# Setting up constants in a planned order: sparse attention and a multiplicative FFN on one Trainium2 core

## Chip, cores and metric

The kernel runs on one core of one Trainium2 chip (trn2). The metric is the device time of one launch in microseconds (us). The core's engines are named as the profile names them: PE (matrix products; its weight loads are listed as PEld), DVE (vector), ACT (scalar and activation), POOL (GpSimd) and SP, whose queue issues the DMA transfers. Each engine takes its own instructions in order and waits for others through semaphores.

## The reference

Two stages. The first is attention over 8 batches, 8 heads, 576 positions and a head size of 64. Heads 0 to 3 see the last 32 positions; heads 4 to 7 see the earlier positions that are congruent modulo 32. The second is an FFN on the 4608 tokens.

```python
scores = scale * np.matmul(q, k.transpose(0, 1, 3, 2))
rel = pos[:, None] - pos[None, :]
mask_local = (rel >= 0) & (rel < stride)                       # stride = 32
mask_strided = (rel >= 0) & (pos[None, :] % stride == pos[:, None] % stride)
attn = softmax(np.where(mask, scores, -1e9))                   # 4 heads each
x = (attn @ v).transpose(0, 2, 1, 3).reshape(B * S, H * D)     # 4608 x 512
a, b = x @ w1, x @ w2                                          # 512 -> 1024
out = ((a * b) @ w3) @ w_out                                   # 1024 -> 1024 -> 512
```

The kernel is given fp32 arrays and computes in fp16 with fp32 accumulation. It forms w3 @ w_out once (called w34) and uses that in place of the last two products.

## The kernel before, in words

**Two layers of code.** First come plain statements that build constants (lines 322 to 387). Then the kernel declares its work as operations of a `Plan`: each has a set of engines with a cost in ns for each, the operations it depends on, buffers that it takes and gives back (4 PSUM banks "f", 2 pairs "B", 7 staging tiles "stg", and others) and a rank. `Plan.order` (line 86) walks a clock: at each moment, each free engine takes the ready operation with the lowest rank. The sequence that comes out is then issued, and every instruction issued through `pin` keeps its place in its engine's program order. The planner's clock decides only this order; on the chip each instruction waits for its real operands. `busy` (line 95) holds the moment at which the planner lets each engine begin.

**Dummy matmuls.** When PE has nothing ready for the next 350 ns of the planner's clock, before 26 us of it, and more than one bank "f" is free, the planner puts in a `spin` (line 326): a 128x512 matmul on the first block of w34, which is zeroed beforehand. It costs the planner 432 ns before 7 us and 216 after.

**Constants.** POOL makes the identity `id16`, the local mask `maskL`, `sel` and `causal`. DVE zeroes the borders of `kTS` and `kTL`, makes `place` from `id16`, and fills columns D to P of the value tiles `v16L` and `v16S` (two of each, for even and odd batches) with ones, which make PV also sum the weights. Two small matmuls at line 371 make the strided mask: the first from `sel`, whose product times `causal` is `maskK`; the second from `place` and `maskK`, whose result is copied to `maskS`. From the masks come `biasL` and `biasS` (line 380). ACT copies the ones into the second value tiles (lines 385 and 387). Only the two mask matmuls are pinned; the order of the other constant instructions is left to the framework, which places them on each engine as the trace shows.

**Main work.** Loads (line 311, SP's queue) bring fp32 tiles into the seven staging tiles in the fixed order of `_loads`: two blocks of w3, q and k of the second group of batch 0, the remainder of batch 0's positions, q and k of the first group, values, another w3 block, four parts of w_out, and so on. POOL casts each to fp16 (line 308), in the same order, which frees the staging tile. On PE then follow:

- `tr` (line 552): transposes of a w3 block; `mm` (line 571): its product with w_out, evicted to w34.
- `T` (line 643): transposes of q and k for a pair of heads; `R` (line 596): the same for the last 64 positions.
- `S` (lines 677 and 686): scores. For the first four pairs a bias matmul adds the mask before ACT's exp; later pairs multiply by the mask after it.
- `X` (lines 724 and 734): weights times values (PV); then a normalisation on DVE, and for some pairs `U` (line 803), a transpose back.
- `a`, `b` (lines 838 and 854): x @ w1 and x @ w2 for tiles of 512 tokens, multiplied on DVE; `o` (line 874): times w34, evicted by ACT and stored.

Of the kernel before, what the change touches and what calls it, by code (L numbers as in the profile page):

```python
# [9 lines left out]
FP32 = mybir.dt.float32  # L10
FP16 = mybir.dt.float16
AF = mybir.ActivationFunctionType
ALU = mybir.AluOpType
# [37 lines left out]
class Plan:  # L51
# [34 lines left out]
    def order(self, slack=0, start=None, spin=None, first=("ACT", "DVE", "POOL")):  # L86
# [5 lines left out]
            for d in o.deps:  # L92
                d.succ.append(o)
        free = {k: [(0, i) for i in range(n)] for k, n in self.cap.items()}
        busy = dict(SP=800, POOL=4200, ACT=3200, DVE=6500, PE=1500)
        busy.update(start or {})
        avail = {e: [] for e in busy}
        for o in ops:
# [5 lines left out]
        t, left = 0, len(ops)  # L104
# [38 lines left out]
        while left:  # L143
            while rel and rel[0][0] <= t:
                w, k, i = heapq.heappop(rel)
# [14 lines left out]
            if busy["SP"] <= t and nxt < len(self.loads):  # L160
                o = self.loads[nxt]
# [10 lines left out]
            for e in ("PE", *first):  # L172
# [3 lines left out]
                for o in avail[e]:  # L176
                    r = ready(o, e)
# [25 lines left out]
                o = best[1]  # L203
# [40 lines left out]
            if nxt < len(self.loads):  # L244
                o = self.loads[nxt]
# [6 lines left out]
            t = min(later)  # L252
# [4 lines left out]
def kernel(  # L257
# [11 lines left out]
    nc = tc.nc  # L269
    cfg = CFG  # L270
    B, H, S, D = q.shape
# [3 lines left out]
    P = 128  # L275
# [7 lines left out]
    SQ, ST = 72, 8  # L283
    NM = 512
    NR = S - NM
    KB = 96
# [6 lines left out]
    psp = ctx.enter_context(tc.tile_pool(name="psp", bufs=1, space=bass.MemoryType.PSUM))  # L293
# [27 lines left out]

    pin(nc.scalar.preload_act_table_set("natural_log_exp_and_others"))
    w34 = consts.tile([P, KF, DM], FP16)
    nc.vector.memset(w34[:, 0, :], 0.0)

    def spin(key):
        ps = bank("f", key, [P, DM], FP32)
# [3 lines left out]
    kTL = consts.tile([P, 2, 32 + S + 32], FP16)  # L331
    kTS = consts.tile([P, 2, ST * KB + 32], FP16)
    v16L = [consts.tile([P, 4, LT, P], FP16, name=f"v16L{i}") for i in range(2)]
    v16S = [consts.tile([KB, 4, ST, P], FP16, name=f"v16S{i}") for i in range(2)]
    ptms = [consts.tile([P, 576], FP16, name=f"ptm{i}") for i in range(4)]
    nc.vector.memset(kTS, 0.0)
    nc.vector.memset(kTL[:, :, 0:32], 0.0)
    id16 = consts.tile([P, P], FP16)
    make_identity(nc, id16)

    idR = consts.tile([P, NR], FP16)
    nc.scalar.copy(out=idR.rearrange("p (g u t) -> p g u t", g=4, u=2),
                   in_=id16[:, 32:32 + NR].rearrange("p (t u g) -> p g u t", u=2, g=4))

    maskL = consts.tile([P, LQ], FP16)
    nc.gpsimd.memset(maskL, 1.0)
# [6 lines left out]
    sel = consts.tile([4, 18, 4], FP16)  # L353
# [4 lines left out]
    causal = consts.tile([SQ, SQ], FP16)  # L358
# [1 line left out]
    nc.gpsimd.affine_select(out=causal, in_=causal, compare_op=ALU.is_ge, fill=0.0, base=0,  # L360
                            pattern=[[1, SQ]], channel_multiplier=-1)
    place = consts.tile([SQ, KB], FP16)
    nc.vector.memset(place, 0.0)
    nc.vector.tensor_copy(out=place[0:64, 32:KB], in_=id16[0:64, 0:64])
    nc.vector.tensor_copy(out=place[64:SQ, 0:32].rearrange("k (i f) -> k f i", f=4)[:, 0], in_=id16[64:SQ, 64:SQ])
    maskK = consts.tile([SQ, SQ], FP16)
    maskS = consts.tile([KB, SQ], FP16)
    sel2 = sel.rearrange("r a b -> r (a b)")
    for i, (lhs, rhs, n) in enumerate(((sel2, sel2, SQ), (place, maskK, KB))):
        mps = psp.tile([P, 512], FP32, tag=f"f{i}", name="mps")  # L370
        pin(nc.tensor.matmul(mps[0:n, 0:SQ], lhs, rhs, start=True, stop=True))
        if i == 0:
            nc.vector.tensor_mul(maskK, mps[0:n, 0:SQ], causal)
        else:
            nc.vector.tensor_copy(out=maskS, in_=mps[0:n, 0:SQ])

    biasL = consts.tile([P, LQ], FP16)
    biasS = consts.tile([KB, SQ], FP16)
    for o, i in ((biasL, maskL), (biasS, maskS)):
        nc.vector.tensor_scalar(out=o, in0=i, scalar1=-1.0, scalar2=30000.0, op0=ALU.add, op1=ALU.mult)  # L380

    nc.vector.memset(v16L[0][:, :, :, D:P], 1.0)  # L382
    nc.vector.memset(v16L[0][0:32, :, 0, :], 0.0)
    nc.vector.memset(v16S[0][:, :, :, D:P], 1.0)  # L384
    nc.scalar.copy(out=v16L[1][:, :, :, D:P], in_=v16L[0][:, :, :, D:P])
    nc.vector.memset(v16L[1][0:32, :, 0, 0:D], 0.0)
    nc.scalar.copy(out=v16S[1][:, :, :, D:P], in_=v16S[0][:, :, :, D:P])

    xT = [consts.tile([P, NTOK], FP16, name=f"xT{cc}") for cc in range(4)]
    w1h = consts.tile([P, KM, DF], FP16)  # L390
# [6 lines left out]
    POOL = {"POOL": 1040}  # L397
# [14 lines left out]
        o.clean = clean if first else 0  # L412
        return o

    early = []

    def cast(name, key, dmas, eng, fn, deps=(), take=(), last=True, rank=10):
        if eng == POOL and len(early) < cfg.get("early", 0):
            eng = {"POOL": 1040, "DVE": 700, "ACT": 1048}
            early.append(key)  # L420
        return plan.op(name, eng, fn, deps=list(dmas) + list(deps), take=take,
                       give=[("stg", key)] if last else [], rank=rank, lock=True)

    CE = cfg.get("cast", {})
    w3c, woc, w1c, w2c, x16, x16op, vop = {}, {}, {}, {}, {}, {}, {}
    Top, Rop, Sop, PVop = {}, {}, {}, {}
# [72 lines left out]
    def load_vL(b, hp):  # L499
        vt = v16L[b % 2]  # L500
        hs = slice(2 * hp, 2 * hp + 2)
        key = f"vL{b}_{hp}"
        ds = []
        ds.append(dma(key, key, 1500, [P, 2, LT, D], lambda s: s[32:P].rearrange("p h t d -> p (h t) d"),
                      _ap(v, (b * H + 2 * hp) * S * D, [[D, LQ], [LQ * D, 2 * LT], [1, D]]), clean=0))
        cs = []
        for i, pr in enumerate((bass.ds(32, 32), bass.ds(64, 64))):
            def fn(e, pr=pr):
                copy(e, vt[pr, hs, :, 0:D], stg[key][pr])
            c = cast(f"c{key}{i}", key, ds, {"POOL": 825}, fn, last=(i == 1))  # L510
            late.append((c, lambda: [PVop.get((b - 2, h, g)) for h in (0, 1) for g in (0, 1)]))
            cs.append(c)
        hl = plan.op(f"h{key}", cfg.get("halo", {"POOL": 660}),
                     lambda e: copy(e, vt[0:32, hs, 1:LT, 0:D], vt[96:P, hs, 0:LT - 1, 0:D]),
                     deps=cs, rank=9, lock=True)
        late.append((hl, lambda: [PVop.get((b - 2, h, g)) for h in (0, 1) for g in (0, 1)]))
        for g in range(2):
            vop[(b, hp, g)] = cs + [hl]
# [23 lines left out]
    for jc in range(KF):  # L542
        js = bass.ds(jc * P, P)
        key = f"tr{jc}"

        def fn(e, jc=jc, key=key):
            if "w3T0" not in big:
                for i in range(2):
                    big[f"w3T{i}"] = ffn.tile([P, KF // 2, DF], FP16, tag="abt", bufs=4, name=f"w3T{i}")
            ps = bank("f", key, [P, KF, P], FP16)  # L550
            for kc in range(KF):
                pin(nc.tensor.transpose(ps[:, kc], big[f"w3_{jc}"][:, bass.ds(kc * P, P)], id16))  # L552

        t = plan.op(key, {"PE": 450}, fn, deps=[w3c[jc]],
                    take=[("f", key)] + ([("abt", "w3T0"), ("abt", "w3T1")] if jc == 0 else []),
                    give=[("w3n", f"w3_{jc}")], rank=cfg["frank"](jc) - 0.3)
        e0 = plan.op(f"w3T0_{jc}", {"DVE": 420, "ACT": 585},
                     lambda e, key=key, js=js: copy(e, big["w3T0"][:, :, js], bank("f", key)[:, 0:4]),
                     deps=[t], rank=5)
        e1 = plan.op(f"w3T1_{jc}", {"ACT": 585, "DVE": 420},  # L560
                     lambda e, key=key, js=js: copy(e, big["w3T1"][:, :, js], bank("f", key)[:, 4:8]),
                     deps=[t, e0], give=[("f", key)], rank=5)
        for nh in range(2):
            mk = f"mm{jc}_{nh}"
            ns = bass.ds(256 * nh, 256)
            h = None
            for hf in range(2):
                def fn(e, hf=hf, mk=mk, js=js, ns=ns):
                    ps = bank("f", mk, [P, 256], FP32) if hf == 0 else bank("f", mk)
                    for kc in range(4 * hf, 4 * hf + 4):  # L570
# [3 lines left out]
                h = plan.op(f"{mk}_{hf}", {"PE": 437}, fn, deps=[(e0, e1)[hf], woc[2 * nh + hf], h],  # L574
                            take=[("f", mk)] if hf == 0 else [], rank=cfg["frank"](jc + nh * cfg.get("nhr", 0)) - 0.1 * hf)
# [11 lines left out]
    prevPV = [None, None]  # L587
    xqs_t = {}
    ptm_t = {}
    for b in range(B):  # L590
        def fnR(e, b=b):
            ps = bank("f", f"R{b}", [P, 512], FP32)
            pv = ps.rearrange("x (i a c t) -> x i a c t", i=2, a=8, c=4)
            for i in range(2):
                for c in range(4):
# [4 lines left out]
                             rank=cfg["arank"](b, 0, "R"), soft=True)  # L600
        Rev = []
# [17 lines left out]
        for pi, hp in enumerate(cfg["pord"](b)):  # L619
# [51 lines left out]
            def fnS(e, hp=hp, nm2=nm2, w=w, m=m, kT=kT, kw=kw, local=local, pm=pm):  # L671
# [8 lines left out]
                for g in range(2):  # L680
                    sps = bank("B", f"S{nm2}_{g}")
                    for i in range(m):
                        ks, qs = kw * (g * m + i), w * (g * m + i)
                        for h in range(2):
# [2 lines left out]
                                                 qT[r_, hp, qs:qs + w], start=not pm, stop=not pm or i == m - 1))  # L687

            s = Sop[(b, hp)] = plan.op(f"S{nm2}", {"PE": (300 if local else 360) + 500 * pm}, fnS,
                                       deps=evs + Rev + prevPV, take=[("B", f"S{nm2}_0"), ("B", f"S{nm2}_1")],  # L690
                                       rank=rank("S"), soft=True, mode=1)
            for g in range(2):
                sk = f"S{nm2}_{g}"
# [43 lines left out]

                if old:
                    fp = fpo
                pv = PVop[(b, hp, g)] = plan.op(pk, {"PE": 246}, fp, deps=[mo] + vop[(b, hp, g)],  # L740
                                                take=[("B", pk)], rank=rank(f"P{g}"), soft=True)
                ptmu[pslot] = pv
                newPV[g] = pv
# [195 lines left out]
```

The softmax here doesn't subtract the row's maximum and nothing guards it: scores larger than these inputs give would overflow.

## Time and profile before

| | us |
|---|---|
| median of 6 runs | 281.04 (280.5 to 281.43) |
| the profiled execution, its time | 281.42 |
| its span in the trace | 279.7 |
| time outside the span | 1.72 |
| PE busy / DVE busy / ACT busy / POOL busy | 268.0 / 173.9 / 173.9 / 118.2 |
| DMA traffic, share of 16 engines | 48.65 MB, 57.2% (queue q1) |

The span runs from the first to the last instruction in the trace; the time of the execution is 1.72 us longer. In the page, busy time is the union of an engine's instruction times. Matmuls are pipelined, so that one matmul's row is longer than the distance to the next one's start: a full engine is seen by its having no idle time, and its pace by the distance of starts. In rows of groups or of the timeline, `out<-in` are the program's names of the tiles, followed by shapes and the number of instructions; the bracket tells how long the engine was idle before and what ended that. A cast's end is its start plus its length.

The first microseconds of the page's slices (40 slices of 7 us) show PE empty in the first and nearly full from the second on:

```profile
PE   0998999999999999999999999999999999999995
```

DVE builds constants in this time, as its timeline shows (start, length, engine, line):

```profile
1.32 0.72 DVE L336 MEMSET kTS<- 128x800 uint32 x1
2.01 0.09 DVE L337 MEMSET kTL<- 128x32 uint32 x1
2.05 0.10 DVE L363 MEMSET place<- 72x48 uint32 x1
2.41 1.34 DVE L382 MEMSET v16L<- 128x1536 f16 x1 [0.27 <-issue]
4.13 1.76 DVE L384 MEMSET v16S<- 96x2048 f16 x1 [0.38 <-issue]
5.89 0.27 DVE L383 MEMSET v16L<- 32x256 uint32 x1
6.13 0.17 DVE L386 MEMSET v16L<- 32x128 uint32 x1
6.23 0.48 DVE L364 COPY place<-id 64x64 f16<-64x64 f16 x1
6.72 0.17 DVE L365 COPY place<-id 8x8 f16<-8x8 f16 x1
6.92 0.19 DVE L380 TENSOR_SCALAR biasL<-maskL 128x96 f16<-128x96 f16 x1
7.02 0.22 DVE L373 TENSOR_TENSOR maskK<-mps,causal 72x72 f16<-72x72 f32 x1
7.55 0.23 DVE L375 CAST maskS<-mps 96x72 f16<-96x72 f32 x1 [0.31 <-PE mps L371]
7.82 0.18 DVE L380 TENSOR_SCALAR biasS<-maskS 96x72 f16<-96x72 f16 x1
```

### The profile page before, as it was taken

How to read it: one execution, taken by the hardware profiler on the slowest of the kernel's cores; microseconds unless marked ns; L12 is line 12 of the kernel's file. 1: busy time of each engine (PE TensorE's matmuls, PEld its weight loads, DVE VectorE, ACT ScalarE, POOL GpSimd, SP SyncE). 2: the span in 40 equal slices, each digit the busy share in tenths (PEclk: the TensorE clock that was granted, in tenths of full speed). 3: DMA queues.
4: the chain of work that ended last, by engine and by line, in shares of the span. 5: the costliest groups of instructions: out<-in, count | busy, mean ns of one | idle time of the engine just before them, and what ended most of it. 6: DMA issues, size and time to landing. Idle time of an engine off the chain costs nothing.

```text
span 279.7 us, 6299 instructions
## 1 busy us (share of the span) xinstructions
PE 268.0 (96%) x2434; PEld 151.7 (54%) x2434; DVE 173.9 (62%) x328; ACT 173.9 (62%) x321; POOL 118.2 (42%) x146
## 2 busy tenths in 40 slices
PE   0998999999999999999999999999999999999995
PEld 0566895746555555555555555555555544444443
DVE  7244756777678757875786778587857773320321
ACT  3454578775668866786677758865885675324321
POOL 6777997699579979550645073100000000000000
PEclk9999999999999999999999999999999999999999
DMA  6999999996999999978275300210020003003003
GB/s 235 355 357 297 364 356 353 266 267 216 301 269 309 302 302 290 273 209 272 82 193 168 147 1 2 98 56 2 1 113 39 2 0 152 1 0 150 0 2 150
DMA packets 53422, 48.65 MB, mean 174 GB/s; under 512 B 20752, under 2 KB 45584, under 8 KB 53392
## 3 DMA queue, kind: packets, MB, share of 16 engines
q1 hardware_dynamic: 53392, 48.24, 57.2%
q8 instruction: 19, 0.31, 0.5%
q14 instruction: 11, 0.09, 0.1%
HBM read 38.80 MB, written 9.44 MB: 172 GB/s over the span
## 4 chain that ended last, share of the span: by engine, by line
PE 95%; DVE 4%; issue 0%; ACT 0%; DVEq 0%
PE ps_o L874 23%; PE ps_b L854 22%; PE ps_a L838 22%; PE ps_T L643 5%; PE ps_mm L571 5%; PE ps_S L686 4%; PE ps_X L734 3%; PE ps_X L724 3%; PE ps_spin L328 2%; PE ps_U L803 2%; PE ps_tr L552 1%; DVE v16S L384 1%; PE ps_R L596 1%; PE ps_S L677 1%; DVE xqs L753 0%; DVE v16L L382 0%
## 5 line engine op out<-in xcount | busy, mean ns | idle before, releaser
L838 PE MATMUL ps_a<-xT,w1h 128*128 128x512 f16 x288 | 73.8, 379 | 0.0
L854 PE MATMUL ps_b<-xT,w2h 128*128 128x512 f16 x288 | 73.8, 379 | 0.0
L860 DVE TENSOR_TENSOR abt<-ps_b,asb 128x512 f16<-128x512 f32 x72 | 49.4, 689 | 39.3 <-PE ps_b L854 38.7
L874 PE MATMUL ps_o<-w,abt 128*128 128x512 f16 (+1 forms) x296 | 67.4, 374 | 0.0
L304 ACT COPY asb<-ps_a 128x512 f32<-128x512 f32 x72 | 42.2, 589 | 40.2 <-PE ps_a L838 39.4
L308 POOL CAST x<-st 128x1024 f16<-128x1024 f32 x32 | 32.9, 1038 | 34.3 <-PE ps_T L643 25.8
L854 PEld LDWEIGHTS <-w2h 128*128 128x128 f16 x288 | 26.9, 98 | 29.2
L874 PEld LDWEIGHTS <-abt 128*128 128x128 f16 x296 | 26.9, 98 | 27.7
L838 PEld LDWEIGHTS <-w1h 128*128 128x128 f16 x288 | 26.5, 98 | 26.6
L704 ACT ACTIVATE ps_S<-ps_S 96x576 f32<-96x576 f32 (+1 forms) x56 | 32.9, 628 | 11.0 <-PE ps_S L686 10.5
L304 ACT COPY osb<-ps_o 128x512 f32<-128x512 f32 x35 | 20.6, 588 | 18.5 <-PE ps_o L874 18.2
L790 DVE TENSOR_TENSOR xT<-ps_X,rcp 64x288 f16<-64x288 f32 x56 | 25.1, 449 | 5.6 <-ACT rcp L774 5.0
L308 POOL CAST v16L<-st 32x768 f16<-32x768 f32 (+1 forms) x32 | 26.3, 823 | 3.5 <-DMA st<-in_v_dram 1.9
L712 DVE TENSOR_TENSOR ptm<-ps_S,maskL 128x576 f16<-128x576 f32 x28 | 19.8, 751 | 12.0 <-ACT ps_S L704 12.0
L753 DVE TENSOR_TENSOR xqs<-ps_X,rcq 96x384 f16<-96x384 f32 (+1 forms) x36 | 20.5, 568 | 1.2
L712 DVE TENSOR_TENSOR ptm<-ps_S,maskS 96x576 f16<-96x576 f32 x28 | 19.8, 748 | 1.3 <-ACT ps_S L704 0.5
L308 POOL CAST v16S<-st 96x1024 f16<-96x1024 f32 x16 | 16.4, 1036 | 6.4 <-PE ps_X L724 6.4
L643 PE MATMUL ps_T<-id,x 128*128 128x128 f16 x256 | 19.1, 219 | 0.0
L774 ACT ACTIVATE rcp<-ps_X 64x576 f32<-64x576 f32 x28 | 18.1, 647 | 0.9
L763 ACT ACTIVATE ps_X<-ps_X 64x576 f32<-64x576 f32 x28 | 17.7, 631 | 0.9 <-PE ps_X L724 0.5
L306 DVE COPY qT<-ps_T 128x512 f16<-128x512 f16 x16 | 11.1, 692 | 9.6 <-PE ps_T L643 8.3
L734 PEld LDWEIGHTS <-ptm 128*96 128x96 f16 (+1 forms) x224 | 14.2, 123 | 4.3
(80 smaller groups left out, 279.3 us busy)
## 6 DMA issues: line engine op xcount, KB each, us to landing
out_dram<-osb SPq DMA_DIRECT2D x35, 256.0 KB
st<-in_moe_w_dram SPq DMA_DIRECT2D x16, 512.0 KB
st<-in_q_dram SPq DMA_DIRECT2D x16, 512.0 KB
st<-in_k_dram SPq DMA_DIRECT2D x16, 512.0 KB
st<-in_v_dram SPq DMA_DIRECT2D x16, 288.0 KB
st<-in_v_dram SPq DMA_DIRECT2D x16, 256.0 KB
st<-in_moe_w_out_dram SPq DMA_DIRECT2D x4, 512.0 KB
st<-in_q_dram SPq DMA_DIRECT2D x8, 128.0 KB
```

Source lines behind the costliest of these rows:

```text
L304: pin(nc.scalar.copy(out=out, in_=in_))
L308: pin(nc.gpsimd.tensor_copy(out=out, in_=in_))
L643: pin(nc.tensor.transpose(ps[:, c * P:(c + 1) * P], x16[(b, x, hp // 2)][:, c, h0:h0 + 2] .rearrange("p h d -> p (h d)"), id16))
L704: pin(nc.scalar.activation(out=sps, in_=sps, func=AF.Exp, bias=0.0, scale=scale))
L712: pin(nc.vector.tensor_mul(ptm[0:kr, 0:576].rearrange("p (h a x) -> p h a x", h=2, x=w), pte[0:kr].rearrange("p h (a x) -> p h a x", x=w), ...
L734: pin(nc.tensor.matmul(xps[0:w, h, i * 65:(i + 1) * 65], ptms[pslot][0:kr, c0:c0 + w], vt[0:kr, 2 * (hp % 2) + h, g * m + i, 0:D + 1], sta ...
L753: pin(nc.vector.tensor_mul(xqs[0:w, 0:m].rearrange("p i h d -> p h i d"), xv[:, :, :, 0:D], _ap(rcp, 0, [[rcp.ap[0][0], w], [4, 2], [1, m] ...
L790: pin(nc.vector.tensor_mul(o, i0, i1))
L838: pin(nc.tensor.matmul(ps, w1h[:, ci, js], xT[ci][:, tok], start=(ci == 0), stop=(ci == KM - 1)))
L854: pin(nc.tensor.matmul(ps, w2h[:, ci, js], xT[ci][:, tok], start=(ci == 0), stop=(ci == KM - 1)))
L860: pin(nc.vector.tensor_mul(big[("abt", t)][:, jc, :], bank("f", f"b{t}_{jc}"), live[("asb", t, jc)]))
L874: pin(nc.tensor.matmul(ps, big[("abt", t)][:, ci, bass.ds(ts * P, P)], w34[:, ci, bass.ds(pt * nw, nw)], start=(ci == 0), stop=(ci == KF - ...
```

## The change

The constants on DVE, ACT and PE become operations of the plan, and their instructions are pinned. POOL's constants stay as they are; an operation `pl` of zero length stands for their end. The planner's start times for POOL, ACT and DVE are set to 3000, 2150 and 1300 ns. Since the mask matmuls are now planned, dummy matmuls can stand ahead of them and between them. S of the first four pairs depends on the biases, and each PV on the ones of its value tile. The helper `on` and its table `ALT` allow a cast to be put on another engine by configuration; the configuration names none. The `early` count, which was 0, goes.

```diff
-        busy = dict(SP=800, POOL=4200, ACT=3200, DVE=6500, PE=1500)
+        busy = dict(SP=800, POOL=3000, ACT=2150, DVE=1300, PE=1500)
...
-    nc.vector.memset(w34[:, 0, :], 0.0)
+    pin(nc.vector.memset(w34[:, 0, :], 0.0))
...
-    nc.vector.memset(kTS, 0.0)
-    nc.vector.memset(kTL[:, :, 0:32], 0.0)
...
-    nc.vector.memset(v16L[0][:, :, :, D:P], 1.0)
-    nc.vector.memset(v16L[0][0:32, :, 0, :], 0.0)
-    nc.vector.memset(v16S[0][:, :, :, D:P], 1.0)
-    nc.scalar.copy(out=v16L[1][:, :, :, D:P], in_=v16L[0][:, :, :, D:P])
-    nc.vector.memset(v16L[1][0:32, :, 0, 0:D], 0.0)
-    nc.scalar.copy(out=v16S[1][:, :, :, D:P], in_=v16S[0][:, :, :, D:P])
+    def first_dve(e):
+        pin(nc.vector.memset(kTS, 0.0))
+        pin(nc.vector.memset(kTL[:, :, 0:32], 0.0))
+        pin(nc.vector.memset(place, 0.0))
+        pin(nc.vector.tensor_copy(out=place[0:64, 32:KB], in_=id16[0:64, 0:64]))
+        pin(nc.vector.tensor_copy(out=place[64:SQ, 0:32].rearrange("k (i f) -> k f i", f=4)[:, 0],
+                                  in_=id16[64:SQ, 64:SQ]))
+
+    def mask_mm(key, lhs, rhs, n):
+        def fn(e):
+            pin(nc.tensor.matmul(bank("f", key, [P, 512], FP32)[0:n, 0:SQ], lhs, rhs, start=True, stop=True))
+        return fn
...
+    def ones(e, i, local):
+        t = v16L[i] if local else v16S[i]
+        if i == 0:
+            pin(nc.vector.memset(t[:, :, :, D:P], 1.0))
+        else:
+            pin(nc.scalar.copy(out=t[:, :, :, D:P], in_=(v16L if local else v16S)[0][:, :, :, D:P]))
+        if local:
+            pin(nc.vector.memset(t[0:32, :, 0, 0:D] if i else t[0:32, :, 0, :], 0.0))
+
+    pl = plan.op("pool", {"POOL": 0}, lambda e: None)
+    d0 = plan.op("init", {"DVE": 1300}, first_dve)
+    plan.op("idR", {"ACT": 310}, lambda e: pin(
+        nc.scalar.copy(out=idR.rearrange("p (g u t) -> p g u t", g=4, u=2),
+                       in_=id16[:, 32:32 + NR].rearrange("p (t u g) -> p g u t", u=2, g=4))))
+    m0 = plan.op("mk0", {"PE": 100}, mask_mm("mk0", sel2, sel2, SQ), deps=[pl, d0], take=[("f", "mk0")], rank=-200)
+    d1 = plan.op("maskK", {"DVE": 230}, lambda e: pin(
+        nc.vector.tensor_mul(maskK, bank("f", "mk0")[0:SQ, 0:SQ], causal)), deps=[m0], give=[("f", "mk0")])
+    m1 = plan.op("mk1", {"PE": 100}, mask_mm("mk1", place, maskK, KB), deps=[d1], take=[("f", "mk1")], rank=-200)
+    d2 = plan.op("maskS", {"DVE": 230}, lambda e: pin(
+        nc.vector.tensor_copy(out=maskS, in_=bank("f", "mk1")[0:KB, 0:SQ])), deps=[m1], give=[("f", "mk1")])
+    biases = [plan.op("bias", {"DVE": 190}, bias(*x), deps=[y]) for x, y in (((biasL, maskL), pl),
+                                                                            ((biasS, maskS), d2))]
+    onesop = {}
+    for local, c0, c1 in ((False, 1780, 1900), (True, 1620, 1500)):
+        onesop[(0, local)] = plan.op("ones", {"DVE": c0}, lambda e, local=local: ones(e, 0, local), deps=[d2], rank=1)
+        onesop[(1, local)] = plan.op("ones", {"ACT": c1}, lambda e, local=local: ones(e, 1, local),
+                                     deps=[onesop[(0, local)]], rank=8)
...
-                                       deps=evs + Rev + prevPV, take=[("B", f"S{nm2}_0"), ("B", f"S{nm2}_1")],
+                                       deps=evs + Rev + prevPV + biases * pm, take=[("B", f"S{nm2}_0"), ("B", f"S{nm2}_1")],
...
-                pv = PVop[(b, hp, g)] = plan.op(pk, {"PE": 246}, fp, deps=[mo] + vop[(b, hp, g)],
+                pv = PVop[(b, hp, g)] = plan.op(pk, {"PE": 246}, fp, deps=[mo, onesop[(b % 2, local)]] + vop[(b, hp, g)],
```

More of the change, by code (lines that the diff above doesn't have):

```diff
@@ L341 @@
     idR = consts.tile([P, NR], FP16)
-    nc.scalar.copy(out=idR.rearrange("p (g u t) -> p g u t", g=4, u=2),
-                   in_=id16[:, 32:32 + NR].rearrange("p (t u g) -> p g u t", u=2, g=4))
     maskL = consts.tile([P, LQ], FP16)
@@ L362 @@
     place = consts.tile([SQ, KB], FP16)
-    nc.vector.memset(place, 0.0)
-    nc.vector.tensor_copy(out=place[0:64, 32:KB], in_=id16[0:64, 0:64])
-    nc.vector.tensor_copy(out=place[64:SQ, 0:32].rearrange("k (i f) -> k f i", f=4)[:, 0], in_=id16[64:SQ, 64:SQ])
     maskK = consts.tile([SQ, SQ], FP16)
     maskS = consts.tile([KB, SQ], FP16)
[L368 to L375, printed above, removed]
@@ L377 @@
     biasL = consts.tile([P, LQ], FP16)
     biasS = consts.tile([KB, SQ], FP16)
-    for o, i in ((biasL, maskL), (biasS, maskS)):
-        nc.vector.tensor_scalar(out=o, in0=i, scalar1=-1.0, scalar2=30000.0, op0=ALU.add, op1=ALU.mult)
-    nc.vector.memset(v16L[0][:, :, :, D:P], 1.0)
-    nc.vector.memset(v16L[0][0:32, :, 0, :], 0.0)
-    nc.vector.memset(v16S[0][:, :, :, D:P], 1.0)
-    nc.scalar.copy(out=v16L[1][:, :, :, D:P], in_=v16L[0][:, :, :, D:P])
-    nc.vector.memset(v16L[1][0:32, :, 0, 0:D], 0.0)
@@ L387 @@
-    nc.scalar.copy(out=v16S[1][:, :, :, D:P], in_=v16S[0][:, :, :, D:P])
+    sel2 = sel.rearrange("r a b -> r (a b)")
+    def first_dve(e):
[5 more added lines that the diff above has]
+                                  in_=id16[64:SQ, 64:SQ]))
@@ new lines, in mask_mm, with bias @@
+    def mask_mm(key, lhs, rhs, n):
+        def fn(e):
+            pin(nc.tensor.matmul(bank("f", key, [P, 512], FP32)[0:n, 0:SQ], lhs, rhs, start=True, stop=True))
+        return fn
+    def bias(o, i):
+        return lambda e: pin(nc.vector.tensor_scalar(out=o, in0=i, scalar1=-1.0, scalar2=30000.0, op0=ALU.add,
+                                                     op1=ALU.mult))
+    def ones(e, i, local):
[6 more added lines that the diff above has]
+            pin(nc.vector.memset(t[0:32, :, 0, 0:D] if i else t[0:32, :, 0, :], 0.0))
@@ L413, in dma, with on @@
         return o
-    early = []
+    ALT = {1040: {"DVE": 700, "ACT": 1048}, 1048: {"DVE": 700, "ACT": 1048}, 1230: {"DVE": 800, "ACT": 1200},
+           825: {"DVE": 560, "ACT": 810}, 660: {"DVE": 590, "ACT": 700}}
+    def on(key, eng):
+        x = cfg.get("ce", {}).get(key)
+        return {x: (POOL["POOL"] if x == "POOL" else ALT[min(eng.values())][x])} if x else eng
     def cast(name, key, dmas, eng, fn, deps=(), take=(), last=True, rank=10):
[L418 to L421, printed above, removed]
+        return plan.op(name, on(name[1:], eng), fn, deps=list(dmas) + list(deps), take=take,
                        give=[("stg", key)] if last else [], rank=rank, lock=True)
@@ L512, in load_vL @@
             cs.append(c)
-        hl = plan.op(f"h{key}", cfg.get("halo", {"POOL": 660}),
+        hl = plan.op(f"h{key}", on(f"h{key}", {"POOL": 660}),
                      lambda e: copy(e, vt[0:32, hs, 1:LT, 0:D], vt[96:P, hs, 0:LT - 1, 0:D]),
```

## The prediction, made before the changed kernel was built

> **What bounds the kernel now.** I read the engine table over three windows, then the waits, the chain of waits of the first 24 us, and the timeline. First the windows: length, then busy us (instructions) of PE, PE weight load, DVE, ACT and POOL, the granted clock, DMA share and GB/s.
>
> ```profile
> 0.00:23.50 23.50, 15.14 (x154) 9.26 (x155) 11.03 (x24) 11.48 (x19) 16.94 (x30) 1.00 0.94 326
> 23.50:269.50 246.00, 245.92 (x2247) 138.67 (x2244) 161.37 (x301) 160.66 (x300) 101.31 (x117) 1.00 0.56 162
> 269.50:279.70 10.20, 6.96 (x41) 3.72 (x38) 1.54 (x3) 1.76 (x3) 0.00 (x0) 0.99 0.27 103
> ```
>
> From 23.5 us on PE has 0.08 us of idle time in 246 us, so nothing can be won there except by starting it earlier. Everything that PE lacks lies in the first 23.5 us. The longest PE wait there, and the chain (start, us, what):
>
> ```profile
> PE mps L371 <- DVE maskK L373: 4.2, 1, 4.2
> ```
>
> ```profile
> 2.41 1.34 DVE v16L L382
> ...
> 4.13 1.78 DVE v16S L384
> ...
> 6.30 0.41 DVE place L364
> ...
> 7.30 0.22 PE mps L371
> 7.52 3.89 PE ps_spin L328 x9
> 11.41 0.85 PE ps_tr L552 x8
> ...
> 13.45 2.59 PE ps_spin L328 x12
> 16.04 0.46 PE ps_T L643 x8
> ```
>
> PE's queue is in order and both mask matmuls stand at its head. The second needs `place` and `maskK`; DVE makes them only after it has filled v16L and v16S with ones, so PE stands until 7.30. Behind it come nine dummy matmuls, 0.43 us each, then the first w3 transposes, more dummies, and the first attention transposes (T) at 15.88. None of this waits for data:
>
> ```profile
> 9.55 1.04 POOL L308 CAST x<-st 128x1024 f16<-128x1024 f32 x1 [0.44 <-DMA st<-in_k_dram]
> ...
> 15.88 1.06 PE L643 MATMUL ps_T<-id,x 128*128 128x128 f16 x16
> ```
>
> T's operands were ready at 9.55 + 1.04 = 10.59; it ran 5.29 us late. The question is how much of this a later limit takes back. I matched every POOL cast, in order, with the first PE row that reads it. The tightest pair:
>
> ```profile
> 25.94 1.04 POOL L308 CAST w3n<-st 128x1024 f16<-128x1024 f32 x1 [1.54 <-PE ps_mm L571]
> ...
> 29.55 1.06 PE L552 MATMUL ps_tr<-id,w3n 128*128 128x128 f16 x16
> ```
>
> The row at 29.55 is two blocks of eight transposes 0.055 us apart; the second block (29.99) reads the fifth w3 cast, ready at 26.98: 3.01 us of slack. The row's "PE" is misleading: the semaphore of this cast's DMA rose at 25.79, long after the transposes that free its buffer, so the cast follows the DMA stream, whose share is 0.94 over the first window. The next tightest: the sixth w3 cast (33.29, read at 36.45: 3.2), the local value halo (29.64, read at 32.97: 3.3), the seventh w3 cast (34.27, 37.59: 3.3), batch 1's remainder (37.36, 40.75: 3.4). From the FFN weights on it is over 4 us, from batch 3 on over 9. So PE runs at least 3.0 us behind its data everywhere.
>
> **The change, part by part.**
>
> *DVE's order.* kTS, kTL and `place` now come first, the fills with ones after `maskS`. From DVE's first row at 0.94: 0.27 + 0.72 + 0.09 + 0.10, then the copies 0.48 + 0.17, with start gaps about 2.9. The first mask product was done at 3.08 already and `causal` is ready at 2.96, so maskK (0.22) ends near 3.4, the second mask matmul (0.22) near 3.8, instead of 7.52: 3.7 us off the head of PE's queue. The fills (1.76 + 1.34 + 0.27 + 0.17 = 3.5) follow maskS and the biases (0.23 + 0.18 + 0.19) and end near 8. Their cover: DVE's first other row stands at 12.30, and the evictions of the first w3 transposes, now due near 6.5, may go to ACT and are first read by the products of line 571, which need wo (first cast done at 17.80). Cost 0; without that cover at most the 1.8 us of one fill. ACT's two copies of ones (1.90 + 1.46) likewise end near 11, before its first T eviction near 11.7; if they slide later, each can hold up an exp by up to its 1.9 us.
>
> One rule speaks against this part. The row: the `place` copy of 64x64 took 0.48 us and ended at 6.71, as the POOL cast beside it ended at 6.68; a larger one-input DVE row (biasL, 128x96) took 0.19. The Trainium skill, "SBUF — State Buffer", section "Who interferes with whom", says that a DVE copy in a two-port mode and GpSimd lock each other out for a whole instruction. The copy now meets POOL's mask selects (0.24 to 0.37 each, the last ending at 2.96). By the row it stays 0.48; by the rule it could wait until 2.96 and end at 3.2, or push a select by as much. I take 0.48; either way 0.3 us lies under the dummies.
>
> *Dummies ahead of the masks.* PE can begin when w is zeroed (1.21) rather than at 7.33. About four 0.43 us dummies fit before 3.1, one between the mask matmuls, three before the first w3 transposes (cast ready at 5.16). They cost at most one dummy, 0.43, of delay, all before 10.59. Do they gain by warming? In the trace dummies start 0.427 us apart until about 13.1 and 0.216 after, although the clock column says 1.00 throughout: 5.8 us of work before full rate. The skill ("TensorE: Matmul & The Clock Gate", "What's actually happening") gives 3.4 us in a free-running window and closes the gate again after an idle window. Counting from 1.3 us, the row puts full rate at 7.1, the rule (one to two windows, my estimate) at 4.7 to 8.1. Both are before T. Were the gate still closed at 8 (the mask gaps counting as idle), some 11 dummies would cost 11 x 0.21 = 2.3 us more, and T would come at 12.4, still 3.5 early. I take 0.
>
> *PE after that.* T at 10.7 (was 15.88, 5.2 earlier); R behind its cast (11.71) at 11.8; its evictions end near 13.6; the first S near 13.7 (was 18.95). The second pair's T needs the cast ending at 14.30 (was 19.32: 4.9 earlier); PV needs v16S at 15.28 (was 20.22: 4.8); the normalisations and second S follow, so U ends near 19.0 (was 23.67). The products of line 571 then need wo3 (20.82) and wo1 (22.27) and run about 4.3 earlier. Then the fifth w3 cast holds: 26.98 plus 0.1 from cast to PE gives 27.08 instead of 29.99, **2.9 us earlier**. Every later slack is larger, so the 2.9 reaches the end.
>
> *Planner.* The new start times (POOL 3000, ACT 2150, DVE 1300) and the constants as planned operations can redraw the static orders. The trace has no row for this. Bounds: a better order fills the hole before 27.08 and is stopped by the next slacks, -4.0; a worse one leaves PE standing, bounded above only by the rivals below. Nearest is the order the trace shows, so 0. The new dependencies (S on biases, PV on ones) are met by 8 us, against S at 13.7. `on` and ALT are inert: CFG has no "ce" entry and early was 0. No DMA is added, moved or removed; SP's queue is the same.
>
> Sum against the profiled execution: span 279.7 - 2.9 = 276.8; its time 281.42 - 2.9 = 278.5. The median shown, 281.04, is 0.38 below that execution, so I forecast **278.1**.
>
> **Rivals.**
> 1. *Better order* (PE fills the hole before 27.08): gain 3.3 to 4.2, say 277.2. For: the hole is about 1.4 us. Against: S of the first local pair needs the normalisation behind it.
> 2. *The cover is gone.* The 5 us of lateness hid every eviction and arrival misjudged in the order; without it small PE waits return between 10 and 45 us and half is lost: 1.5 gained, 279.5. Against: the slacks above are measured arrivals.
> 3. *Hidden anyway or not done*: arrivals after 23 us set the end, 281.0. Against: 3.0 us of slack at every load.
> 4. *Slower.* An instruction needing a late cast is ordered into PE's queue ahead of work that is ready: for instance the last w3 block (cast 45.14) ahead of the first FFN products (ready at 40.3) holds PE 4.8 us. Before 27 us such a stand costs little, since PE must wait for the fifth w3 cast anyway; after it, one longer than 2.9 makes the kernel slower: with 4.8, 281.0 + 1.9 = 282.9. For: the lists are redrawn as a whole, and a stand this long was invisible while PE was late.
>
> **How the numbers follow.** Chances: forecast 0.62 (277.6 to 278.6), better order 0.12, cover gone 0.11, hidden 0.05, slower 0.10. Faster by over 0.2% (0.56 us, about what a measurement can tell): 0.62 + 0.12 + 0.11 = 0.85; same 0.05; slower 0.10. The range 277.0 to 280.4 leaves out the far part of the better order (0.03), hidden and slower (0.15).
>
> **What would show it.** Right: no DVE wait over 1 us on PE's second mask matmul, dummies from 1.3 us, T at 10.6 to 10.9, the fifth w3 block right behind its cast at 27.1, PE full from there, the last row 2.9 earlier. Wrong: T later than 12.5 (clock or fills), POOL casts later than before (the port), or PE gaps after 27 us (order).

## The result, and the profile after

The changed kernel takes 279.53 us (median; 278.51 to 281.89 in 31 runs) against 280.78 us (279.8 to 281.55 in 68 runs): ratio 0.9963, 95% interval 0.9953 to 0.9972. It is faster by 1.0 us by the ratio, 1.25 by the medians. Forecast was 2.9. The profiled executions differ by more than the medians: 279.06 us with a span of 277.3, against 281.42 with 279.7. Two executions in the experiments below, 305.82 us at a granted clock of 0.88 (experiment 3) and 288.71 us at 0.95 (kernel before), ran in a slower state of the chip and are left out of the medians and ratios.

The windows of the changed kernel (columns as before):

```profile
0.00:23.50 23.50, 18.05 (x184) 10.92 (x185) 13.31 (x27) 12.37 (x20) 16.32 (x29) 1.00 0.93 325
23.50:267.00 243.50, 242.59 (x2212) 135.63 (x2210) 159.78 (x298) 159.87 (x298) 101.95 (x118) 1.00 0.56 164
```

PE is busy 2.9 us more in the first window, and it now stands idle 0.91 us after it, where it had 0.08. Apart from 1.3 us at the very start, until w is zeroed, its largest waits in the first 30 us are (in total, times, longest):

```profile
PE ps_tr L575 <- POOL w3n L308: 2.1, 4, 0.9
PE ps_mm L594 <- POOL woh L308: 1.1, 1, 1.1
PE ps_spin L328 <- DVE w3T L306: 0.9, 1, 0.9
```

No wait for the masks is left. PE waits for casts of loaded data, and once for a bank that DVE frees late because the fills with ones stand in front (the third line; the part on DVE's order below says why they stood there so late). In time, from the timeline:

```profile
1.27 1.89 PE L328 MATMUL ps_spin<-w 128*128 128x512 f16 x4 [1.27 <-DVE w L324]
...
3.75 0.22 PE L375 MATMUL ps_mk<-maskK,place 72*96 72x72 f16 x1
...
10.74 1.06 PE L666 MATMUL ps_T<-id,x 128*128 128x128 f16 x16
...
26.35 1.04 POOL L308 CAST w3n<-st 128x1024 f16<-128x1024 f32 x1 [1.16 <-DMA st<-in_moe_w_dram]
...
27.45 0.62 PE L575 MATMUL ps_tr<-id,w3n 128*128 128x128 f16 x8 [0.91 <-POOL w3n L308]
```

The second mask matmul is issued at 3.75 and T at 10.74, 5.14 us earlier than before. The fifth w3 block stands directly behind its cast: ready at 26.35 + 1.04 = 27.39, read at 27.45. The chain of waits goes back from there not to DVE but to the stream of loads:

```profile
17.07 9.14 DMA st<-in_moe_w_dram
...
26.35 1.05 POOL w3n L308
...
27.45 0.62 PE ps_tr L575 x8
```

The engine line of the chain was "PE 95%; DVE 4%" before; it is now:

```profile
PE 89%; DMA 7%; POOL 1%; SPq 1%; issue 0%; DVE 0%; POOLq 0%; DVEq 0%
```

So the mechanism is the one forecast, down to the block that holds PE. The size is not.

### The profile page after: what moved, and what is told of

It is laid out like the page before. It is cut to its first block, busy times and chain, and to the rows that moved or that the text cites. A ratio compares the mean times of both kernels' runs of the same rounds, so it can differ in the third digit from the quotient of the medians.

```text
span 277.3 us, 6298 instructions
## 1 busy us (share of the span) xinstructions
PE 267.7 (97%) x2433; PEld 150.3 (54%) x2433; DVE 174.6 (63%) x328; ACT 174.0 (63%) x321; POOL 118.3 (43%) x146
## 4 chain that ended last, share of the span: by engine, by line
PE 89%; DMA 7%; POOL 1%; SPq 1%; issue 0%; DVE 0%; POOLq 0%; DVEq 0%
PE ps_o L897 23%; PE ps_b L877 23%; PE ps_a L861 22%; PE ps_T L666 5%; DMA st<-in_moe_w_dram 5%; PE ps_S L709 4%; PE ps_mm L594 3%; PE ps_X L757 3%; PE ps_X L747 3%; PE ps_U L826 2%; DMA st<-in_k_dram 2%; SPq L311 1%; PE ps_tr L575 1%; POOL w3n L308 1%; PE ps_R L619 1%; POOL v16S L308 0%
## 5 line engine op out<-in xcount | busy, mean ns | idle before, releaser
L594 PE MATMUL ps_mm<-woh,w3T 128*128 128x256 f16 x128 | 15.9, 272 | 1.1 <-POOL woh L308 1.1
```

Source lines behind the costliest of these rows:

```text
L594: pin(nc.tensor.matmul(ps, big[f"w3T{kc // 4}"][:, kc % 4, js], big["woh"][:, kc, ns], start=(kc == 0), stop=(kc == KF - 1)))
```

## The experiments

**A constant to read all of them by.** In every profile of the kernel before, the time less the start of the fifth w3 block on PE was 251.41 to 251.45 us, and the time less the start of the first T was 265.52 to 265.55. After that block PE is full, so each microsecond by which it starts later is a microsecond at the end. In these six profiles (the first, one in experiment 1, four in experiment 7) it starts when PE gets to it; in the changed kernel it starts when its data is there.

**1. Both kernels again.** No edit; one profile each.

> The kernel before, unchanged, profiled once more. Landing theory (after the change PE follows the casts, and the end moves with the landings between 20 and 34 us; before it, PE is late by its dummies, whose pace depends on when the PE clock opens): the time moves with the start of the first attention transposes T, which was 15.88 in the profile at 281.42 us, so about 265.5 us plus that start; a typical run has T nearer 15.2. The landing of the first local value tile (27.05 in the first profile) scatters by half a microsecond or more without moving the time. Contention theory (the change itself makes the casts after 20 us later): that landing stays within 0.2 us of 27.05.

> The changed kernel, unchanged, profiled once more. Landing theory: its time is about 251.3 us plus the landing of the first local value tile (27.76 at 279.06 us), and this landing differs from 27.76 by some tenths up to 1 us either way. Contention theory: the landing is again 27.7 or later, and at least 0.5 later than in the kernel before on the same chip.

Measured: 280.65 for the kernel before, T at 15.12 (265.5 + 15.12 = 280.6), the fifth w3 cast ready at 27.88, not 26.98. The changed kernel took 281.13 us, more than every profile of the kernel before but the first. Its timeline:

```profile
28.61 1.04 POOL L308 CAST w3n<-st 128x1024 f16<-128x1024 f32 x1 [1.01 <-DMA st<-in_moe_w_dram]
...
29.70 0.62 PE L575 MATMUL ps_tr<-id,w3n 128*128 128x128 f16 x8 [1.43 <-POOL w3n L308]
```

The same program, the same order, T at 11.77, and the fifth w3 cast ready at 29.65 instead of 27.39. 251.43 + 29.70 = 281.13: the landing is the time. I had tied the time to the first local value tile's landing; the fifth w3 block describes it better. Only the first profile of the changed kernel stands off, by 0.18 us (279.06 - 27.45 = 251.61), most of it from a later cast, the sixth w3 block, ready at 34.00 and read at 34.06. The marks named beforehand did not decide between the theories. The cast of the first local value tile began at 27.99 in the kernel before (27.17 in its first profile), so it scatters, as the landing theory has it. In the changed kernel it began at 29.71, 1.7 us later on the same chip: that is the mark of the contention theory, and more than the landing theory allowed.

**2. DVE's order alone.** The kernel before, constants pinned in the new order, everything else as it was; all dummies thus stand behind the masks.

```diff
-    nc.vector.memset(place, 0.0)
-    nc.vector.tensor_copy(out=place[0:64, 32:KB], in_=id16[0:64, 0:64])
+    pin(nc.vector.memset(place, 0.0))
+    pin(nc.vector.tensor_copy(out=place[0:64, 32:KB], in_=id16[0:64, 0:64]))
...
-    nc.vector.memset(v16L[0][:, :, :, D:P], 1.0)
+    pin(nc.vector.memset(v16L[0][:, :, :, D:P], 1.0))
```

> Kernel before with DVE's constants pinned in the new order alone (kTS, kTL, place, masks, biases, then the ones); planner, start times and dummies as before, so that all dummies stand behind the mask matmuls. Landing theory: masks done near 3.8, nine dummies from there, T near 11.8 (11.4 to 12.7) instead of 10.7; the later waits for data absorb this, so the time is that of the changed kernel: 1.0 to 1.3 us under before (ratio 0.995 to 0.997). Rival (dummies ahead of the masks and planned constants carry the gain): less than half of it, ratio 0.998 or more.

Measured: 279.48 us, ratio 0.9967 (0.9951 to 0.9984). T came at 12.69, two microseconds later than in the changed kernel, and the fifth w3 block at 28.28, behind its cast (28.23): 251.43 + 28.28 = 279.71, this profile's time. The interval holds the changed kernel's 0.9963: pinning DVE's constants in another order is enough for the gain, and nothing else in the change is needed for it.

**3. Dummies taken away**, from the kernel before and from the changed one.

```diff
-           first=('DVE', 'ACT', 'POOL'), early=0, pm=4,
+           first=('DVE', 'ACT', 'POOL'), early=0, spin=False, pm=4,
```

> Kernel before without any dummy matmul; the constants in their old order, so PE still waits 4.2 us for the second mask matmul, until 7.3. Landing theory: the w3 transposes run at once after it, T comes with its cast at 10.7 but at half clock, T to S take 1 to 2 us longer, most of which the waits for data before 27 us absorb: 0.3 to 1.2 us under before (ratio 0.9957 to 0.999). Rival (the wait for the masks is itself the loss): the time of before, ratio 1.000, or slower by the cold clock.

> Changed kernel without any dummy matmul, so that only the early masks remain. Landing theory: T comes with its cast near 10.3 but at half clock, as in the kernel before without dummies, and from there both are the same program: the fifth w3 block right behind its cast, time about 251.4 us plus its start, ratio to before 0.996 to 0.9985. Rival (dummies ahead of the masks carry the gain): ratio 1.000 or more.

Measured: without dummies the kernel before took 279.94 us, ratio 0.9982 (0.9959 to 1.0004), which points the expected way but doesn't exclude no change, and so doesn't exclude its rival. The changed kernel without dummies took 279.68, ratio 0.9963 (0.9951 to 0.9975): the same as with them. Its profile shows what the dummies do (it is that of an execution of 280.15 us):

```profile
20.60 6.39 PE L594 MATMUL ps_mm<-woh,w3T 128*128 128x256 f16 x40
...
28.26 1.08 PE L575 MATMUL ps_tr<-id,w3n 128*128 128x128 f16 x16
```

Forty products take 6.39 us where the kernel before needed 4.78 (its row at 23.50): they start 0.213 us apart up to 23.8 us and 0.109 after. Yet the fifth w3 block starts at 28.72, 0.06 behind its cast. PE spends the slack that it has won on a slow clock, and the end does not see it.

**4. PE made late again.** 14 and 22 more dummies just before the first T of the changed kernel (the edit is shown with 14).

```diff
     def spin(key):
         ps = bank("f", key, [P, DM], FP32)
-        pin(nc.tensor.matmul(ps, w34[:, 0, 0:P], w34[:, 0, :], start=True, stop=True))
+        spins.append(key)
+        for _ in range(1 + 14 * (len(spins) == 21)):
+            pin(nc.tensor.matmul(ps, w34[:, 0, 0:P], w34[:, 0, :], start=True, stop=True))
```

> Changed kernel with 14 more dummies (14 x 0.216 = 3.0 us) just before the first T, which then starts near 13.8 instead of 10.7. Landing theory: the fifth w3 cast (ready between 27.0 and 29.6 in five profiles) still comes after PE's own progress (265.5 + 13.8 = 279.3 us if PE alone set the end), so the 3.0 us cost 0 to 0.4 us: ratio to before 0.996 to 0.998. Rival (PE's early progress sets the end): 3.0 us more than the changed kernel, about 282.5, ratio 1.006.

> The same with 22 more dummies (4.75 us), T near 15.5. Landing theory: now PE is late in nearly every run and its progress sets the end: 265.5 + 15.5 = 281.0 us, ratio to before 1.000 to 1.003, and a smaller scatter than the changed kernel's, as the landings no longer count. Rival as before: 4.75 us more than the changed kernel, about 284.3, ratio 1.012.

Measured: with 14, 279.7 us, ratio 0.9972 (0.9956 to 0.9989); 3.0 us of delay cost 0.2 by the medians. With 22, 280.92 us, ratio 1.0002 (0.9989 to 1.0015): the gain is gone. The timelines, first with 14, then with 22:

```profile
13.71 1.06 PE L670 MATMUL ps_T<-id,x 128*128 128x128 f16 x16
...
27.22 1.04 POOL L308 CAST w3n<-st 128x1024 f16<-128x1024 f32 x1 [1.42 <-PE ps_mm L598]
...
28.32 0.62 PE L579 MATMUL ps_tr<-id,w3n 128*128 128x128 f16 x8 [0.34 <-POOL w3n L308]
```

```profile
14.61 1.06 PE L670 MATMUL ps_T<-id,x 128*128 128x128 f16 x16
...
27.07 1.04 POOL L308 CAST w3n<-st 128x1024 f16<-128x1024 f32 x1 [0.85 <-PE ps_mm L598]
...
28.27 1.06 PE L579 MATMUL ps_tr<-id,w3n 128*128 128x128 f16 x16
```

With T at 13.71 PE still stands 0.34 us before the block. With T at 14.61 it runs the fourth and fifth block together (the second eight start at 28.71), 0.6 us after the cast was ready at 28.11. The step between held by data and held by PE thus lies between a T at 13.7 and one at 14.6, for a landing as in these runs. With 22 dummies the times fall into two groups, 280.12 to 280.14 (4 runs) and 280.88 to 281.00 (10 runs); each is far narrower than the changed kernel's 3.4 us between lowest and highest. T was expected at 15.5 and came at 14.61 in this profile, which belongs to the first group. The traces show what fits the split. In this profile DVE begins biasS just before POOL begins its first cast:

```profile
4.26 0.18 DVE L383 TENSOR_SCALAR biasS<-maskS 96x72 f16<-96x72 f16 x1
4.30 1.04 POOL L308 CAST w3n<-st 128x1024 f16<-128x1024 f32 x1 [1.35 <-DMA st<-in_moe_w_dram]
```

With 14 dummies the cast began at 4.20, before biasS, which then took 1.01 us; everything behind it on DVE came 0.8 us later, and PE waited 0.73 us for a bank that DVE frees, a wait that the profile with 22 does not have. Eight more dummies on top of T at 13.71 give 13.71 + 8 x 0.216 = 15.44, and 265.52 + 15.44 = 280.96, inside the second group. This is an estimate; no profile of the second group is on record.

**5. Less data in front.** The changed kernel, with three of the four w_out loads cut to 16 partitions. It leaves out most of w_out, so w34 is formed from what the staging tiles held before, and the output is not the reference's.

```diff
-        d = dma(key, key, 1530, [P, 4, 256], lambda s: s, src)
+        d = dma(key, key, 1530, [P, 4, 256], lambda s: s if g == 2 else s[0:16], src if g == 2 else src[0:16])
```

> Changed kernel with the same order of instructions, but three of the four w_out loads bring 16 of 128 partitions (w34 is then computed from what the staging tiles held): 1.3 MB less in front of the fifth w3 block, some 3.9 us at 340 GB/s. Landing theory: that cast is ready near 24.2 instead of 28, so PE's own progress (T near 10.8: 265.5 + 10.8 = 276.3) or another load sets the end: 276.3 to 277.8 us, ratio to before 0.984 to 0.990, and scatter below that of the changed kernel. Rival (the missing part of the gain was spent by the change itself): no faster than the changed kernel, ratio 0.996.

Measured: 277.96 us, ratio 0.9919 (0.9895 to 0.9943): faster than the changed kernel by 1.6 us, with the order of PE's instructions unchanged. The scatter did not shrink (277.42 to 280.32), and the time is just outside the range expected (276.3 to 277.8). The timeline says why:

```profile
19.79 4.99 PE L594 MATMUL ps_mm<-woh,w3T 128*128 128x256 f16 x40 [1.13 <-POOL woh L308]
...
23.62 2.02 POOL L308 CAST w3n<-st 128x1024 f16<-128x1024 f32 x2
...
26.05 1.06 PE L575 MATMUL ps_tr<-id,w3n 128*128 128x128 f16 x16
```

The fifth w3 cast was ready at 25.65, 1.7 us earlier than in the changed kernel rather than 3.9. It no longer holds PE, whose second eight transposes start at 26.50 (251.43 + 26.50 = 277.93). But PE was late from its wait of 1.13 us for w_out, up to 19.79, which I had left out when I took T + 265.5.

**6. Another order of loads and copies.** The sixth and seventh w3 blocks loaded ahead of batch 0's local values, and four copies of these values moved from POOL to ACT and DVE by the new configuration; each alone, both together, and with all four on ACT.

```diff
-        ('vL', 0, 0), ('vL', 0, 1), ('w3', 5), ('w3', 4),
+        ('w3', 5), ('w3', 4), ('vL', 0, 0), ('vL', 0, 1),
...
+           ce=dict(vL0_00='ACT', vL0_10='ACT', hvL0_0='DVE', hvL0_1='DVE')
```

> Changed kernel with one change in the order of loads: the sixth and seventh w3 blocks ahead of batch 0's two local value tiles, so that POOL's two value casts with halo (2.5 us each) no longer stand between the fifth and the sixth w3 cast. Landing theory: the fifth w3 cast still holds PE, so 0 to 0.6 us less than the changed kernel, ratio to before 0.994 to 0.9965; if the late value tiles hold PE instead, slower than the changed kernel by up to 1 us.

> Changed kernel with four of POOL's value copies of batch 0 moved by configuration: the two first casts to ACT, the two halo copies to DVE. POOL gains 3.1 us between the fifth and the sixth w3 cast. Landing theory: the fifth w3 cast is as late as before and still holds PE, and what follows it waited only 0 to 0.2 us more: ratio to before 0.995 to 0.9965, the changed kernel's time within 0.3 us. If POOL's chain set the end: 0.5 us or more below the changed kernel.

> Both together: the sixth and seventh w3 blocks loaded ahead of the local values, and the four copies off POOL. With the later load order the fifth w3 cast was ready at 26.23, and POOL's chain then held batch 1's T (cast ready at 37.12, read at 37.28). Landing theory: with 3.1 us less on POOL that hold goes, 0.5 to 1.2 us below the changed kernel, ratio to before 0.992 to 0.9945. Rival: the copies hold up ACT's and DVE's evictions instead, no gain.

> The same with all four copies on ACT (0.8 and 0.7 us each). The same gain if POOL's chain was the hold; less by up to 0.5 us if ACT's exps are then late.

None showed the gain expected, and none beats the changed kernel. The load order alone took 279.98 us (ratio 0.9974, 0.9961 to 0.9986), 0.45 slower than the changed kernel; a loss of up to 1 us was the other outcome named, though by another wait. In its profile the fifth w3 block ran at 26.28, but batch 1's T then waited for the casts behind the value copies (cast pair, and T at its end):

```profile
35.11 2.02 POOL L308 CAST x<-st 128x1024 f16<-128x1024 f32 x2
...
37.28 0.61 PE L666 MATMUL ps_T<-id,x 128*128 128x128 f16 x8
```

With the copies moved and the old load order: 280.47 us (0.9993, 0.9977 to 1.0008). Both, with halos on DVE: 280.32 (0.9985, 0.9972 to 0.9997); all on ACT: 279.59 (0.9973, 0.9958 to 0.9988). In the first of these three the fifth w3 block was again held by its cast, and another stand had appeared:

```profile
28.08 0.62 PE L576 MATMUL ps_tr<-id,w3n 128*128 128x128 f16 x8 [1.11 <-POOL w3n L309]
...
40.30 0.61 PE L595 MATMUL ps_mm<-woh,w3T 128*128 128x256 f16 x4 [0.61 <-DVE kTS L307]
```

The order was drawn anew, and a w3 product now stands behind an eviction of kTS that is 0.61 us late. This is the rival of redrawn orders at work, in kernels other than the one forecast.

**7. When does the fifth w3 block land in the kernel before?** Four more profiles, no edit.

> Kernel before, unchanged: when is the fifth w3 cast ready (its start is the landing of that load)? So far 26.98 and 27.88 in it, and 27.39, 29.64, 28.66, 28.26 and 28.11 in kernels with the changed constants. Draw theory (26.98 was an early draw of one common scatter): the four new profiles have their middle at 27.9 to 28.5, some above 28.2. Contention theory (the changed constants make the casts later): their middle is at 27.6 or below, none above 28.2. The time is again 251.43 us plus the start of the fifth w3 block on PE in both.

> As for the run before it: a further profile of the kernel before.

> As for the two runs before it: a further profile of the kernel before.

> As for the three runs before it: a further profile of the kernel before.

| kernel before, profile | time | T | fifth w3 cast ready | PE reads it |
|---|---|---|---|---|
| the first | 281.42 | 15.88 | 26.98 | 29.99 |
| experiment 1 | 280.65 | 15.12 | 27.88 | 29.23 |
| 7, first | 280.41 | 14.89 | 27.25 | 29.00 |
| 7, second | 280.03 | 14.51 | 28.45 | 28.62 |
| 7, third | 280.12 | 14.60 | 27.78 | 28.70 |
| 7, fourth | 280.17 | 14.62 | 27.57 | 28.72 |

The middle of the four new ones, and of all six, is 27.68: above what the contention theory allowed, with one above 28.2, and below what the draw theory asked. In five profiles of the changed kernel, whatever its dummies, it is 28.26 (27.39, 28.11, 28.26, 28.66, 29.65); the profiles of experiment 2 (28.23) and of the moved copies with the old load order (28.02) lie there too. So 26.98 was the earliest of thirteen, and the slack of the kernel before is 0.2 to 3.0 us, not 3.0. Whether the changed constants add some tenths to the landing stays open. The two sets overlap, but only one of the six is above 28.0 and only one of the seven below it. The chip is another possible cause: four of the seven come from a chip on which no landing of the kernel before was taken.

## Why the prediction was wrong in size

*What bounds the kernel.* Right: PE full after 23.5 us, late by the masks and the dummies behind them, and the fifth w3 block as the first limit behind. Experiments 1 and 4 show that the time is that block's start plus a constant.

*DVE's order.* Right: second mask matmul near 3.8 (3.75), no wait for the masks left. The lock between DVE and POOL was taken too lightly. The row's 0.48 us of the `place` copy was no length of its own: in the six profiles of the kernel before the copy took 0.31 to 0.58 us and ended 0.03 us after the POOL cast beside it each time. The rule of the Trainium skill ("SBUF — State Buffer", "Who interferes with whom"), which the prediction set against the row, says the same: the later instruction waits for the whole of the earlier one. In the changed kernel both copies (0.21 and 0.31 us) end 0.03 after one of POOL's short selects, which costs nothing. But biasS, summed at 0.18, now meets the first cast:

```profile
4.25 1.04 POOL L308 CAST w3n<-st 128x1024 f16<-128x1024 f32 x1 [1.28 <-DMA st<-in_moe_w_dram]
4.26 1.06 DVE L379 TENSOR_SCALAR biasS<-maskS 96x72 f16<-96x72 f16 x1
```

That puts the fills 0.9 us later. The fills were said to cost nothing; behind biasS they held a dummy's bank for 0.86 us and T with it (cast ready at 10.10, T at 10.74). With data as the limit the later waits absorb this; with 22 more dummies ahead of T it fits the 0.8 us between the two groups.

*Dummies and the clock.* Right that in the changed kernel they cost and gain nothing at the end: experiment 3. The estimate from the rule of the Trainium skill ("TensorE: Matmul & The Clock Gate", "What's actually happening"), full rate at 4.7 to 8.1 us, held in the first profile, where the transposes at 5.34 start 0.056 us apart. In the second neither it nor the row's 7.1 held: dummies started 0.43 us apart up to 10.3 us, 9 us after the first one, and T came at 11.77.

*Planner.* Right: PE's order from the first transposes to the fifth w3 block is the old one. Behind it the slacks nearly carried over: the sixth w3 block, said to have 3.2 us, was at its limit too, because its cast came 0.71 us later than in the first profile.

*The sum.* Here the step "26.98 plus 0.1 from cast to PE gives 27.08 instead of 29.99, **2.9 us earlier**" failed, in both terms. Against the medians, by the constant 251.43 (an estimate: one profile of the changed kernel had 251.61):

| fifth w3 block on PE | prediction | from the medians | error of the gain |
|---|---|---|---|
| before | 29.99 | 280.78 - 251.43 = 29.35 | -0.64 |
| after | 27.08 | 279.53 - 251.43 = 28.10 | -1.02 |
| gain | 2.91 | 1.25 | -1.66 |

The first error, the start before: the first profile came from one of the slowest executions (281.42 in 279.8 to 281.55). I saw 0.38 us of this and subtracted it from the forecast, as if it were common to both kernels. It belongs to the kernel before alone: there the dummies lie on PE's path and the clock sets their pace, while the end of the changed kernel hangs on the landing. In the six profiles of the kernel before PE comes to full pace about 3.3 to 5.8 us after its first dummy, and T follows 7.2 to 8.6 us after it, both latest in the first profile. There the w3 transposes were still slow; in the second profile of experiment 7 they already run at full pace, and T comes 1.37 us earlier. A row of the first profile, then that one:

```profile
11.20 1.06 PE L552 MATMUL ps_tr<-id,w3n 128*128 128x128 f16 x8
```

```profile
7.28 3.69 PE L328 MATMUL ps_spin<-w 128*128 128x512 f16 x9
10.80 0.61 PE L552 MATMUL ps_tr<-id,w3n 128*128 128x128 f16 x8
...
11.91 2.75 PE L328 MATMUL ps_spin<-w 128*128 128x512 f16 x12
14.51 1.06 PE L643 MATMUL ps_T<-id,x 128*128 128x128 f16 x16
```

The second error, the start after: a landing taken from one profile was used as a date. While PE is late, the landing does not move the time and its scatter cannot be seen; once PE waits for it, all of the scatter is in the time. Of the 1.02 us, 27.68 - 26.98 = 0.70 is the distance of that one draw from the middle of the kernel before's own six; the rest, 0.3, is within what stayed open: scatter, the changed constants, or the chip.

*Rivals.* "Hidden anyway" was given 0.05 for its "3.0 us of slack at every load". In the six profiles that slack was 0.2 to 3.0, so that arrivals do hide part of the gain: by the table 1.0 us of the 2.9. "Cover gone" named the right place, 10 to 45 us, and nearly the right time, 279.5, but another mechanism: not misjudged orders, but landings that vary. "Slower" as a stand of an early-ordered instruction did not occur. The range held the time; the likeliest value did not.

## What to carry to other kernels

When a wait is taken from an engine that is late, the gain ends at the next limit; if that limit is a DMA landing, read it from several profiles, and take its middle, not the one at hand. Look also at how the engine's own lateness varies: a start that hangs on how fast the clock opens has a scatter that the change removes on one side only. A difference between two full-engine timelines can often be reduced to the start of one instruction plus a constant; that constant turns each further profile into a measurement of the cause.

## What the runs showed of the hardware

The fifth w3 block is the same 512 KB load, at the same place of the same queue, and its cast was ready between 26.98 and 29.65 us in thirteen profiles of kernels with the same order of loads. Part of the scatter is there when the load is issued (16.24 to 17.81 us, once an earlier cast has freed its staging tile). Why it scatters was not found.

The granted-clock column read 1.00 in the first windows of every profile shown, while matmuls of equal shape started 0.427 us apart early and 0.216 later. The change of pace came about 5.8 us after the first dummy in the first profile, about 3.7 in the changed kernel's first, and about 9 in its second. The distance of starts tells the pace; the column did not.

Slowly clocked PE work can be free: without dummies, 40 products took 6.39 instead of 4.78 us and the kernel's time was the same.

A DVE instruction can wait for a POOL cast that began just before it. In nine profiles with the constants in the plan and biasS at 4.26 us, biasS took 0.93 to 1.06 us, ending 0.03 to 0.04 us after the cast, in the six in which the cast began at 4.12 to 4.25; it took 0.18 in the three in which the cast began at 4.30 to 4.87. A few hundredths of a microsecond in a landing thus move DVE, and where PE waits for DVE's bank, T, by 0.8 us.
